# The key cache read one batch at a time in 4 KB runs, in place of two interleaved batches in 8 KB runs

## The chip, the cores and the metric

The kernel runs on one core of one Trainium2 chip. The metric is the time in microseconds of one execution on the device; lower is better. Each kernel is run several times, and the median is compared.

## The reference

Two transformer-like layers are applied twice, with the same weights both times, to four single-token rows `x` of 512 numbers (B = 4, one query position, 32 query heads in 8 groups, head size 128). Of the cache of 8,192 positions only the last W = 2,048 are used.

```python
def _A_ref(x, k_cache, v_cache, wq, wo):
    q = (x @ wq).reshape(B, Sq, Hq, Dh)            # then (B, Hq, Sq, Dh)
    k = jnp.repeat(k_cache[:, :, Sk - W:, :], rep, axis=1)
    v = jnp.repeat(v_cache[:, :, Sk - W:, :], rep, axis=1)
    scores = jnp.einsum("bhqd,bhkd->bhqk", q, k) * (Dh ** -0.5)
    p = _softmax(scores, axis=-1)
    o = jnp.einsum("bhqk,bhkd->bhqd", p, v)
    return o.transpose(0, 2, 1, 3).reshape(B, Sq, Hq * Dh) @ wo

def _B_ref(x, w_gate, w_up, w_down):
    h = _sigmoid(x @ w_gate) * (x @ w_up)
    return h @ w_down

x = x + _A_ref(_layernorm(x), k_cache, v_cache, wq, wo)
x = x + _B_ref(_layernorm(x), w_gate, w_up, w_down)
x = x + _A_ref(_layernorm(x), k_cache, v_cache, wq, wo)
x = x + _B_ref(_layernorm(x), w_gate, w_up, w_down)
```

For one (batch, head group) pair the used part of K, and likewise of V, is 2,048 x 128 numbers in bf16, 512 KB, contiguous in the device's memory. There are 32 such pairs. wq is 512 x 4096 (4 MB), wo 4096 x 512 (4 MB), the three GLU weights 512 x 1792 each (1.8 MB).

## The kernel before

**Memory.** One big tile, `arena`, is cut into NS = 50 slots of 128 partitions x 2,048 bf16 (512 KB each). A slot holds one (batch, head) block of K or V, or a chunk of a weight. `_SlotPool` hands out free slots in the order in which they were released. The list `loads` holds the transfers to come in their fixed order; `fill()` issues them as long as slots are free, and `done(name)` releases a slot after its last use. Every transfer is issued by SyncE through one line (`dma`, L372), in one queue. Its completion is signalled on one of 24 semaphores in turn, so a transfer also waits for the transfer 24 places earlier.

**Order of the loads.** wq first (four transfers of 1 MB, whole rows of 8 KB, into pairs of slots), then K of the first two units, then for each unit K of the unit two ahead, its wo chunk and its four V blocks. After the eight units come the GLU weights, wq again in 512 KB chunks, V again in reverse order of the units (29 of 32 blocks, since three are kept), and the GLU weights again. K stays in its slots from the first attention to the second, and so do the eight chunks of wo.

**A unit** is one head group with its four batches; there are eight units in each attention. For a unit, `front` does the following. In the first attention only, `k_transpose` (L664 to L670) turns each K slot in place on VectorE, in 32 x 32 blocks of 4-byte words. `softmax_unit` then spreads q into a block form (`q_unit`, L643), computes the scores on TensorE (L689: 16 matmuls of 512 columns, four for each batch, the batches in four groups of 32 columns of the array), takes maxima on VectorE (L697 to L703), and applies the exponential on ScalarE into `prow` (L706). `turn_p` permutes the rows with a matmul (L715), copies them on ScalarE (L717) and transposes on VectorE (L721). `pv_unit` (L755) multiplies with V, 16 matmuls for each V block, and `wo_unit` (L785) with wo. `front` runs two units ahead of `pv_unit`. In the second attention the units run in reverse order, and K's four slots are released right after each unit's scores.

**K before.** Slots 0 to 31 are set aside for K: `pool.free` starts at 32 (L353), head h has slots 4h to 4h+3 (`kpair`, L408), and K needs no slot from the pool, so that `take_k` (L383) issues a K load at once when it is the next in the list. `load_k` (L412) makes two transfers for each head, one for each pair of batches:

```python
src = A_k[2 * bp:2 * bp + 2, h, SK - W:SK, :].rearrange("b (p j) d -> p b (j d)", p=64)
dma("K%d_%d" % (h, bp), kpair(h, bp), src, ..., rate="bw_8k")
```

The even partitions of a pair of slots thus hold one batch and the odd ones the other, each partition 32 consecutive positions (8 KB). The matmuls at L689 pick one batch out of the transposed pair (`b % 2`) with a step of four bf16; the exponential (L706) and the copy (L717) use access patterns that bring the positions back into the order in which V lies (V: 16 consecutive positions in each partition, 4 KB).

**Order of the instructions.** `_schedule` (L86) builds each engine's order from estimated durations and dependencies (its table `tm` has a rate for 8 KB runs and one for 4 KB runs), and `_assign_sync` (L174) sets the semaphore waits.

Of the kernel before, what the change touches and what calls it, by code (L numbers as in the profile page):

```python
# [6 lines left out]
F32 = mybir.dt.float32  # L7
# [265 lines left out]
def build(nc, A_x, A_k, A_v, A_wq, A_wo, B_wg, B_wu, B_wd, out, cfg=None):  # L273
# [40 lines left out]
    with es:  # L314
# [35 lines left out]

        P = _Plan()
        pool = _SlotPool(NS)
        pool.free = list(range(4 * HKV, NS))  # L353
        SB = (0, 1)
        PB = 2
        OBS = (3, 4)
# [23 lines left out]
        loads = []  # L380
        where = {}

        def take_k():  # L383
            while loads and loads[0][0][0] == "K":
                loads.pop(0)[1](None)

        def take_load():
            take_k()
            name, emit = loads.pop(0)
            s = pool.alloc()  # L390
            where[name] = s
            emit(s)

        def fill():
            take_k()
            while loads and pool.free:
                take_load()
                take_k()

        def need(name):  # L400
            while name not in where:
# [2 lines left out]

        def done(name):
            pool.release(where.pop(name))

        def kpair(h, bp):  # L408
            o = (4 * h + 2 * bp) * SLOT
            return arena[:, o:o + 2 * SLOT]  # L410

        def load_k(h):  # L412

            where[("K", h)] = h
            for bp in range(2):
                src = A_k[2 * bp:2 * bp + 2, h, SK - W:SK, :].rearrange("b (p j) d -> p b (j d)", p=64)
                dma("K%d_%d" % (h, bp), kpair(h, bp), src, w=[("slot", 4 * h + 2 * bp + i) for i in range(2)],
                    rate="bw_8k")

        def load_kv(name, cache, b, h):  # L420
            loads.append((name, lambda s: dma(str(name), slot_ap(s), kv_d(cache, b, h), w=[("slot", s)])))
# [55 lines left out]

        def load_wq_rows(c):
            def emit(s):
                assert pool.alloc() == s + 1 and s >= 4 * HKV  # L480
# [181 lines left out]
            return [[(h, b) for h in range(u * nh, (u + 1) * nh) for b in g] for u in range(HKV // nh)]  # L662

        def k_transpose(pairs):  # L664
            h = pairs[0][0]
            need(("K", h))
            for t in range(4):
                v32 = slot_ap(4 * h + t).bitcast(F32)
                P.op("vector", "T%d_%d" % (h, t), c_dve(1024), lambda v, v32=v32: v.transpose(v32, v32),  # L669
                     r=[("slot", 4 * h + t)], w=[("slot", 4 * h + t)])  # L670

        ucount = [0]

        def softmax_unit(tag, pairs):
            u = ucount[0]
            ucount[0] += 1
            k2 = u % 2
            bank = SB[k2]
            ob = OBS[k2]
            hk = pairs[0][0]  # L680
            q_unit(tag, int(tag[0]), pairs[0][0], k2)

            def e_s(pe):
                last = None
                for cp in range(4):
                    for gi, (h, b) in enumerate(pairs):
                        kt = kpair(hk, b // 2).rearrange("p (j c x i t) -> p c t i j x", c=2, x=16, i=2, t=2)
                        q0 = ((k2 * NB + b) * 4 + cp) * NR
                        last = pe.matmul(ps[32 * gi:32 * gi + NR, bank, :], qbd[:, q0:q0 + NR],  # L689
                                         kt[:, cp // 2, cp % 2, b % 2, :, :], start=(cp == 0), stop=(cp == 3))  # L690
                return last
            P.op("tensor", "S" + tag, 16 * tm["pe_row"], e_s,
                 r=[("slot", 4 * hk + t) for t in range(4)] + [("q", k2, a) for a in range(4)],
                 w=[("pss", k2)], banks=(bank,))
            mk = mxt[:, k2 * 32:(k2 + 1) * 32]
            P.op("vector", "mx" + tag, c_dve(512),
                 lambda v: v.tensor_reduce(nmax[:, k2:k2 + 1], ps[:, bank, :], AXX, ALU.max),  # L697
                 r=[("pss", k2)], w=[("mx", k2)], banks=(bank,))
            P.op("vector", "mk" + tag, tm["dve_small"],
                 lambda v: v.tensor_scalar(mk, maskr[:, :], nmax[:, k2:k2 + 1], None, ALU.add),  # L700
                 r=[("mx", k2), ("maskr",)], w=[("mk", k2)])
            P.op("vector", "nm" + tag, tm["dve_small"],
                 lambda v: v.tensor_reduce(nmax[:, 2 + k2:3 + k2], mk, AXX, ALU.max, negate=True, apply_transpose=True),  # L703
                 r=[("mk", k2)], w=[("nm", k2)])
            P.op("scalar", "ex" + tag, c_act(512) + 200.0,
                 lambda a: a.activation(prow[:, :].rearrange("p (m x t) -> p m x t", x=16, t=2),  # L706
                                        ps[:, bank, :].rearrange("p (m t x) -> p m x t", x=16, t=2), ACTF.Exp, bias=nmax[:, 2 + k2:3 + k2], scale=1.0,
                                        accum_out=psm[:, k2:k2 + 1]),
                 r=[("pss", k2)] + [("nm", k2)], w=[("prow",), ("psm", k2)], banks=(bank,))
            return k2  # L710

        def turn_p(tag, k2):
            ob = OBS[k2]
            P.op("tensor", "pp" + tag, tm["pe_sq"],
                 lambda pe: pe.matmul(ps[:, PB, :], perm[:, :], prow[:, :], start=True, stop=True),  # L715
                 r=[("prow",), ("perm",)], w=[("ppb",)], banks=(PB,))
            P.op("scalar", "pc" + tag, c_act(512), lambda a: a.copy(prow[:, :].rearrange("p (m y t) -> p m y t", y=2, t=2),  # L717
                                  ps[:, PB, :].rearrange("p (y m t) -> p m y t", y=2, t=2)),
                 r=[("ppb",)], w=[("prow",)], banks=(PB,))
            P.op("vector", "pt" + tag, c_dve(256),  # L720
                 lambda v: v.transpose(ebuf[:, k2 * 256:(k2 + 1) * 256], prow[:, :].bitcast(F32)),  # L721
                 r=[("prow",)], w=[("e", k2)])
# [71 lines left out]
        def attn(L, gi_, wb):  # L794
# [218 lines left out]
```

## Time and profile before

| | |
|---|---|
| median of 4 runs | 189.49 us (188.82 to 190.07) |
| the profiled execution, its own time | 188.62 us |
| span of that execution, first to last instruction | 186.8 us |
| bytes moved | 72.65 MB, mean 389 GB/s |
| K: 16 transfers of 1,024 KB, to landing (median) | 14.8 us |
| V: 61 transfers of 512 KB, to landing (median) | 14.9 us |
| VectorE K transposes (L669), 32 | 38.0 us, 1,219 ns each |
| TensorE score matmuls (L689), 256 | 32.4 us, 632 ns each |
| ScalarE exponentials (L706) and copies (L717), 16 each | 687 ns and 585 ns each |
| TensorE clock granted, mean | 0.705 |

The profile is one execution. The row of 40 slices shows each engine's busy share in tenths, the DMA row the mean busy share of the sixteen DMA engines, and the row below it the rate in GB/s. A group's line gives the source line, engine, operation, output and input, shape and count, then busy time and mean duration, then the engine's idle time before it and what ended that. Durations of matmuls that run in several column groups at once overlap.

### The profile page before, as it was taken

To read this page: it belongs to the slowest core of one execution; us is meant where nothing else is said; L and a number is where in the kernel's file an instruction comes from. 1 tells how busy PE (TensorE), PEld (TensorE's weight loads), DVE (VectorE), ACT (ScalarE), POOL (GpSimd) and SP (SyncE) were. 2 spreads that over 40 slices of the span, in tenths; PEclk is the share of its full clock that TensorE was granted. 3 is DMA by queue.
4 is the path that set the end of the run, shared out by engine and by line. 5 is a ranking of instruction groups with operands and counts; after the bars stand their busy time and mean duration, and the time that the engine had idled before them with its cause. 6 is when DMAs were issued, how large, how long until landed. Compare 5 with 4: busy or idle time off the path is not lost.

```text
span 186.8 us, 4440 instructions
## 1 busy us (share of the span) xinstructions
PE 101.7 (54%) x1920; PEld 56.5 (30%) x1920; DVE 86.2 (46%) x215; ACT 32.7 (18%) x95; POOL 13.9 (7%) x73
## 2 busy tenths in 40 slices
PE   0433406456607163171644346455989999956543
PEld 0101002312404132040334331321355555655122
DVE  6109999268583854738510031123584443311211
ACT  2000021223303003020020001001463333210200
POOL 3000001101101001010010000000121111100000
PEclk9999996885556758585585555555999699675555
DMA  4999999999999999999999999999999999999990
GB/s 162 419 423 430 424 408 396 422 387 415 408 394 427 384 417 408 398 423 388 396 402 387 405 409 366 405 369 410 409 412 404 406 412 403 408 405 408 403 379 24
DMA packets 20532, 72.65 MB, mean 389 GB/s; under 512 B 1944, under 2 KB 6048, under 8 KB 17952
## 3 DMA queue, kind: packets, MB, share of 16 engines
q1 hardware_dynamic: 20512, 72.37, 97.9%
q8 instruction: 15, 0.25, 0.5%
q14 instruction: 5, 0.04, 0.1%
HBM read 72.36 MB, written 0.00 MB: 387 GB/s over the span
## 4 chain that ended last, share of the span: by engine, by line
DMA 38%; SPq 32%; PE 18%; DVE 6%; issue 2%; ACT 2%; ACTq 0%
SPq L372 32%; DMA arena<-in_A_k_cache_dram 16%; DMA arena<-in_B_w_down_dram 11%; PE ps L689 9%; DMA arena<-in_A_v_cache_dram 6%; DMA arena<-in_A_wq_dram 4%; PE ps L755 3%; DVE arena L669 3%; ACT prow L706 1%; PE ps L715 1%; DVE nmax L697 1%; PE ps L785 1%; PE ps L845 1%; PE ps L877 1%; PE ps L615 1%
## 5 line engine op out<-in xcount | busy, mean ns | idle before, releaser
L689 PE MATMUL ps<-arena,qbd 128*16 128x512 bf16 x256 | 32.4, 632 | 26.7 <-DVE arena L669 21.9
L669 DVE STREAM_TRANSPOSE arena<-arena 128x1024 f32<-128x1024 f32 x32 | 38.0, 1219 | 2.8 <-DMA arena<-in_A_k_cache_dram 2.6
L755 PE MATMUL ps<-ebuf,arena 128*128 128x4 bf16 x1024 | 32.2, 165 | 11.1 <-DMA arena<-in_A_v_cache_dram 10.6
L755 PEld LDWEIGHTS ps<-ebuf,arena 128*128 128x128 bf16 x1024 | 29.7, 100 | 19.1 <-DMA arena<-in_A_v_cache_dram 13.0
L689 PEld LDWEIGHTS ps<-arena,qbd 128*16 128x16 bf16 x256 | 6.7, 99 | 40.2 <-DVE arena L669 22.4
L697 DVE TENSOR_REDUCE nmax<-ps 128x1 f32<-128x512 f32 x16 | 11.0, 685 | 16.2 <-PE ps L689 16.2
L706 ACT ACTIVATE prow<-ps,nmax 128x512 bf16<-128x512 f32 x16 | 11.0, 687 | 36.3 <-DVE nmax L703 26.4
L767 DVE TENSOR_TENSOR onb<-ps,rinv 128x16 bf16<-128x16 f32 x16 | 3.1, 195 | 30.8 <-PE ps L755 30.7
L656 ACT CAST qbd<-ps 32x64 bf16<-32x64 f32 x32 | 6.5, 204 | 55.1 <-DVE qbd L653 35.8
L725 POOL CAST s<-psm 128x1 bf16<-128x1 f32 x16 | 3.0, 186 | 143.7 <-ACT prow L706 143.7
L715 PE MATMUL ps<-prow,perm 128*128 128x512 bf16 x16 | 6.8, 428 | 12.3 <-ACT prow L706 12.1
L615 PE MATMUL ps<-arena,xn 128*4 128x512 bf16 x64 | 8.2, 580 | 8.3 <-DMA arena<-in_A_wq_dram 5.4
L717 ACT CAST prow<-ps 128x512 bf16<-128x512 f32 x16 | 9.4, 585 | 8.7 <-PE ps L715 8.7
L845 PE MATMUL ps<-arena,xn 128*4 128x448 bf16 x64 | 7.3, 556 | 6.1 <-DMA arena<-in_B_w_up_dram 3.3
L721 DVE STREAM_TRANSPOSE ebuf<-prow 128x256 f32<-128x256 f32 x16 | 7.1, 442 | 7.6 <-ACT prow L717 7.5
L785 PE MATMUL ps<-onb,arena 128*128 128x4 bf16 x256 | 9.1, 165 | 2.8 <-issue 1.7
L785 PEld LDWEIGHTS ps<-onb,arena 128*128 128x128 bf16 x256 | 8.0, 100 | 3.3 <-issue 2.9
L653 DVE CAST qbd<-ps 32x64 bf16<-32x64 f32 x32 | 6.7, 210 | 3.8 <-ACT qbd L656 2.5
L623 DVE STREAM_TRANSPOSE ebuf<-ps 128x512 f32<-128x512 f32 x4 | 2.9, 714 | 10.3 <-PE ps L615 10.1
L582 ACT ACTIVATE lnv<-lnv 128x4 f32<-128x4 f32 x4 | 0.8, 206 | 38.1 <-DVE lnv L579 38.1
L852 DVE STREAM_TRANSPOSE ebuf<-ps 128x448 f32<-128x448 f32 x4 | 2.6, 650 | 9.9 <-PE ps L845 9.9
L877 PE MATMUL ps<-hT,arena 128*128 128x4 bf16 x112 | 4.2, 167 | 4.9 <-DVE hT L867 2.5
(55 smaller groups left out, 61.0 us busy)
## 6 DMA issues: line engine op xcount, KB each, us to landing
arena<-in_A_v_cache_dram SPq DMA_DIRECT2D x61, 512.0 KB, 14.9
arena<-in_A_k_cache_dram SPq DMA_DIRECT2D x16, 1024.0 KB, 14.8
arena<-in_A_wq_dram SPq DMA_DIRECT2D x4, 1024.0 KB, 8.0
arena<-in_A_wo_dram SPq DMA_DIRECT2D x8, 512.0 KB, 15.5
arena<-in_A_wq_dram SPq DMA_DIRECT2D x8, 512.0 KB, 7.9
arena<-in_B_w_gate_dram SPq DMA_DIRECT2D x8, 448.0 KB, 13.9
arena<-in_B_w_up_dram SPq DMA_DIRECT2D x8, 448.0 KB, 13.4
arena<-in_B_w_down_dram SPq DMA_DIRECT2D x6, 512.0 KB, 7.1
```

Source lines behind the costliest of these rows:

```text
L372: o = P.op("sync", name, 0.0, lambda e, dst=dst, src=src: e.dma_start(dst, src), r=r, w=w, dma_bytes=nbytes, dma_rate=tm[rate])
L615: last = pe.matmul(ps[32 * hh:32 * hh + NB, qb, :], xn[:, c * NB:(c + 1) * NB], slot_ap(s)[:, hh * 512:(hh + 1) * 512], start=(c == 0), st ...
L669: P.op("vector", "T%d_%d" % (h, t), c_dve(1024), lambda v, v32=v32: v.transpose(v32, v32), r=[("slot", 4 * h + t)], w=[("slot", 4 * h + t)])
L689: last = pe.matmul(ps[32 * gi:32 * gi + NR, bank, :], qbd[:, q0:q0 + NR], kt[:, cp // 2, cp % 2, b % 2, :, :], start=(cp == 0), stop=(cp = ...
L697: lambda v: v.tensor_reduce(nmax[:, k2:k2 + 1], ps[:, bank, :], AXX, ALU.max),
L706: lambda a: a.activation(prow[:, :].rearrange("p (m x t) -> p m x t", x=16, t=2), ps[:, bank, :].rearrange("p (m t x) -> p m x t", x=16, t ...
L715: lambda pe: pe.matmul(ps[:, PB, :], perm[:, :], prow[:, :], start=True, stop=True),
L717: P.op("scalar", "pc" + tag, c_act(512), lambda a: a.copy(prow[:, :].rearrange("p (m y t) -> p m y t", y=2, t=2), ps[:, PB, :].rearrange(" ...
L721: lambda v: v.transpose(ebuf[:, k2 * 256:(k2 + 1) * 256], prow[:, :].bitcast(F32)),
L755: last = pe.matmul(ps[:, ob, gi * REP:(gi + 1) * REP], src[:, j * 128:(j + 1) * 128], ev[:, j % 2, j // 2, gi * REP:(gi + 1) * REP], start ...
L785: last = pe.matmul(ps[:, wb, c * nb:(c + 1) * nb], slot_ap(s)[:, r_ * D + c * 128:r_ * D + (c + 1) * 128], ov[:, o0:o0 + nb], start=(first ...
L845: last = pe.matmul(ps[32 * g:32 * g + NB, SB[n], 0:NF], xn[:, c * NB:(c + 1) * NB], slot_ap(s)[:, g * NF:(g + 1) * NF], start=(c == 0), st ...
```

## The change

K is handled as V is: one transfer of 512 KB for each (batch, head) pair, 16 consecutive positions (4 KB) in each of 128 partitions, into one slot taken from the common pool when the load's turn comes. The 32 set-aside slots, `take_k`, `kpair` and `load_k` go; all 50 slots are in the pool from the start. The order of the loads is the same, with four K transfers of a unit where there were two. `k_transpose` works on the same number of slots. The score matmuls read a step of two bf16 from one slot, the exponential writes in steps of two, and the copy after the row permutation becomes plain. In the second attention the four slots of a unit are released at the same point as before.

```diff
-        pool.free = list(range(4 * HKV, NS))
...
-        def load_k(h):
-
-            where[("K", h)] = h
-            for bp in range(2):
-                src = A_k[2 * bp:2 * bp + 2, h, SK - W:SK, :].rearrange("b (p j) d -> p b (j d)", p=64)
-                dma("K%d_%d" % (h, bp), kpair(h, bp), src, w=[("slot", 4 * h + 2 * bp + i) for i in range(2)],
-                    rate="bw_8k")
...
         def k_transpose(pairs):
-            h = pairs[0][0]
-            need(("K", h))
-            for t in range(4):
-                v32 = slot_ap(4 * h + t).bitcast(F32)
-                P.op("vector", "T%d_%d" % (h, t), c_dve(1024), lambda v, v32=v32: v.transpose(v32, v32),
-                     r=[("slot", 4 * h + t)], w=[("slot", 4 * h + t)])
+            for (h, b) in pairs:
+                s = need(("K", h, b))
+                v32 = slot_ap(s).bitcast(F32)
+                P.op("vector", "T%d_%d" % (h, b), c_dve(1024), lambda v, v32=v32: v.transpose(v32, v32),
+                     r=[("slot", s)], w=[("slot", s)])
...
-                        kt = kpair(hk, b // 2).rearrange("p (j c x i t) -> p c t i j x", c=2, x=16, i=2, t=2)
+                        kt = slot_ap(ks[gi]).rearrange("p (j c k t) -> p c t j k", c=2, k=32, t=2)
                         q0 = ((k2 * NB + b) * 4 + cp) * NR
                         last = pe.matmul(ps[32 * gi:32 * gi + NR, bank, :], qbd[:, q0:q0 + NR],
-                                         kt[:, cp // 2, cp % 2, b % 2, :, :], start=(cp == 0), stop=(cp == 3))
+                                         kt[:, cp // 2, cp % 2, :, :], start=(cp == 0), stop=(cp == 3))
...
-                 lambda a: a.activation(prow[:, :].rearrange("p (m x t) -> p m x t", x=16, t=2),
-                                        ps[:, bank, :].rearrange("p (m t x) -> p m x t", x=16, t=2), ACTF.Exp, bias=nmax[:, 2 + k2:3 + k2], scale=1.0,
+                 lambda a: a.activation(prow[:, :].rearrange("p (j k t) -> p j t k", k=32, t=2),
+                                        ps[:, bank, :].rearrange("p (j t k) -> p j t k", k=32, t=2), ACTF.Exp, bias=nmax[:, 2 + k2:3 + k2], scale=1.0,
...
-            P.op("scalar", "pc" + tag, c_act(512), lambda a: a.copy(prow[:, :].rearrange("p (m y t) -> p m y t", y=2, t=2),
-                                  ps[:, PB, :].rearrange("p (y m t) -> p m y t", y=2, t=2)),
+            P.op("scalar", "pc" + tag, c_act(512), lambda a: a.copy(prow[:, :], ps[:, PB, :]),
...
-                    for t in range(4):
-                        pool.release(4 * us[ui][0][0] + t)
+                    for p in us[ui]:
+                        done(("K",) + p)
...
-            for u in us[0:2]:
-                loads.append((("K", u[0][0]), lambda _, h=u[0][0]: load_k(h)))
+            for (h, b) in us[0] + us[1]:
+                load_kv(("K", h, b), A_k, b, h)
             for ui, pairs in enumerate(us):
                 if ui + 2 < len(us):
-                    loads.append((("K", us[ui + 2][0][0]), lambda _, h=us[ui + 2][0][0]: load_k(h)))
+                    for (h, b) in us[ui + 2]:
+                        load_kv(("K", h, b), A_k, b, h)
```

The new loads use the function that V's loads had already:

```python
def load_kv(name, cache, b, h):
    loads.append((name, lambda s: dma(str(name), slot_ap(s), kv_d(cache, b, h), w=[("slot", s)])))
```

with `kv_d` (L310) giving `cache[b, h, SK - W:SK, :]` as 128 partitions of 16 positions.

More of the change, by code (lines that the diff above doesn't have):

```diff
@@ L381, in build @@
         where = {}
-        def take_k():
-            while loads and loads[0][0][0] == "K":
-                loads.pop(0)[1](None)
         def take_load():
-            take_k()
             name, emit = loads.pop(0)
@@ L394, in fill @@
         def fill():
-            take_k()
             while loads and pool.free:
                 take_load()
-                take_k()
         def need(name):
@@ L406, in done @@
             pool.release(where.pop(name))
-        def kpair(h, bp):
-            o = (4 * h + 2 * bp) * SLOT
-            return arena[:, o:o + 2 * SLOT]
-        def load_k(h):
-            where[("K", h)] = h
-            for bp in range(2):
-                src = A_k[2 * bp:2 * bp + 2, h, SK - W:SK, :].rearrange("b (p j) d -> p b (j d)", p=64)
-                dma("K%d_%d" % (h, bp), kpair(h, bp), src, w=[("slot", 4 * h + 2 * bp + i) for i in range(2)],
-                    rate="bw_8k")
         def load_kv(name, cache, b, h):
@@ L479, in emit @@
             def emit(s):
-                assert pool.alloc() == s + 1 and s >= 4 * HKV
+                assert pool.alloc() == s + 1
                 where[(("wq", c, 1), 0)] = s + 1
@@ L679, in softmax_unit @@
             ob = OBS[k2]
-            hk = pairs[0][0]
+            ks = [where[("K", h, b)] for (h, b) in pairs]
             q_unit(tag, int(tag[0]), pairs[0][0], k2)
@@ L686, in e_s @@
                     for gi, (h, b) in enumerate(pairs):
-                        kt = kpair(hk, b // 2).rearrange("p (j c x i t) -> p c t i j x", c=2, x=16, i=2, t=2)
+                        kt = slot_ap(ks[gi]).rearrange("p (j c k t) -> p c t j k", c=2, k=32, t=2)
                         q0 = ((k2 * NB + b) * 4 + cp) * NR
                         last = pe.matmul(ps[32 * gi:32 * gi + NR, bank, :], qbd[:, q0:q0 + NR],
-                                         kt[:, cp // 2, cp % 2, b % 2, :, :], start=(cp == 0), stop=(cp == 3))
+                                         kt[:, cp // 2, cp % 2, :, :], start=(cp == 0), stop=(cp == 3))
                 return last
             P.op("tensor", "S" + tag, 16 * tm["pe_row"], e_s,
-                 r=[("slot", 4 * hk + t) for t in range(4)] + [("q", k2, a) for a in range(4)],
+                 r=[("slot", s) for s in ks] + [("q", k2, a) for a in range(4)],
                  w=[("pss", k2)], banks=(bank,))
```

## The prediction

> **What bounds the kernel now.** I read first the engines' busy shares and the 40 slices. No compute engine is busy for more than 54% of the span, while the row of the DMA engines stands at 9 from the second slice to the one before the last, with rates between 366 and 430 GB/s.
>
> ```profile
> PE 101.7 (54%) x1920; PEld 56.5 (30%) x1920; DVE 86.2 (46%) x215; ACT 32.7 (18%) x95; POOL 13.9 (7%) x73
> ...
> DMA  4999999999999999999999999999999999999990
> GB/s 162 419 423 430 424 408 396 422 387 415 408 394 427 384 417 408 398 423 388 396 402 387 405 409 366 405 369 410 409 412 404 406 412 403 408 405 408 403 379 24
> ...
> q1 hardware_dynamic: 20512, 72.37, 97.9%
> ```
>
> The third row says the same for the whole span: the packets of SyncE's queue fill 97.9% of sixteen engines' time. So the end is set by how many bytes pass and at which rate. The rate must then be read by kind of run, from windows in which one kind is alone. The columns are: stretch, length, busy time of PE, PEld, DVE, ACT, POOL, granted clock, DMA share, GB/s.
>
> ```profile
> 10.00:24.00 14.00, 4.89 (x64) 1.09 (x64) 9.52 (x13) 0.41 (x2) 0.00 (x0) 1.00 1.01 426
> 26.00:107.00 81.00, 37.82 (x752) 22.78 (x752) 44.41 (x84) 13.76 (x38) 6.04 (x32) 0.64 1.03 403
> 107.00:126.00 19.00, 9.35 (x136) 4.82 (x136) 4.22 (x20) 1.57 (x7) 0.00 (x0) 0.50 1.01 388
> 130.00:166.00 36.00, 34.45 (x732) 19.96 (x728) 17.36 (x63) 13.86 (x39) 6.09 (x32) 0.88 1.03 408
> 134.00:136.00 2.00, 2.00 (x21) 0.47 (x17) 1.67 (x5) 1.06 (x4) 0.75 (x4) 1.00 1.04 416
> ```
>
> From 10 to 24 us only 8 KB runs land (the end of wq and the first six K transfers): 426 GB/s. From 130 to 166 us nearly all is V in 4 KB runs: 408 GB/s. Between 26 and 107 us K, V and wo (1 KB runs) are mixed: 403. From 107 to 126 us, around the first GLU, few slots are free and the rate falls to 388. The share is at 1 in all of them: the engines are never empty, even in the stage from 130 us where PE is busy for 34.45 of 36 us.
>
> Last I read the issues and the end of the chain of waits:
>
> ```profile
> arena<-in_A_v_cache_dram SPq DMA_DIRECT2D x61, 512.0 KB, 14.9
> arena<-in_A_k_cache_dram SPq DMA_DIRECT2D x16, 1024.0 KB, 14.8
> ...
> arena<-in_A_wo_dram SPq DMA_DIRECT2D x8, 512.0 KB, 15.5
> ```
> ```profile
> 168.15 14.62 DMA arena<-in_B_w_down_dram
> 182.81 0.59 PE ps L877 x16
> 183.44 0.39 PE ps L877 x8
> 184.09 0.60 PE ps L940 x4
> 184.71 0.41 DVE prow L943
> ```
>
> A transfer lands some 15 us after its issue, so about 15 x 0.408 = 6 MB stand in the queue. The span ends with the last w_down transfer, about 4 us of fixed work behind it. A microsecond more of DMA time anywhere ahead moves the end by a microsecond.
>
> **The change, part by part.** (1) K comes in 32 transfers of 512 KB in 4 KB runs, not 16 of 1,024 KB in 8 KB runs. The bytes stay: 16 x 1,024 KB = 16.78 MB. At 426 GB/s they take 39.4 us, at V's 408 they take 41.1: +1.7 us. No trace shows K in 4 KB runs, so bounds: V's best short window above has 416 GB/s, 40.3 us, +0.9; the mixed stretch, which wo's 1 KB runs slow down, has 403, 41.6 us, +2.2. I take 408, since V's transfers have the same size, the same runs and the same kind of source. These rates include the completion of each transfer, so the doubled number is in them.
>
> The Trainium skill has two rules here. "DMA: Bandwidth & Descriptors", section "Rules for kernel authors", wants at least 1 MiB a transfer, and the fit of the same page's "Anatomy of one DMA", made for GpSimd's queue, is 2.0 us + bytes / 436 GB/s: 32 x 3.2 - 16 x 4.4 = some 32 us more if each stood alone. V's row speaks against it: 512 KB transfers at 408 GB/s, a queue of 6 MB in front. The section "Why small descriptors are slow" of that page charges about 3 cycles of 32 B beats for each packet: 2 x (128 + 3) against 256 + 3 cycles, 1.2%, an estimate of +0.5 us, below what the windows show.
>
> (2) SyncE issues 16 more transfers. A K issue takes 624 ns in the median, so 16 x 0.62 = 10 us of SyncE's time. In the first stretch six of them push wo's issue from 7.2 to about 11 us, and the first V behind it; that V's issue stalled from 7.9 to 15.8 us on the full queue anyway, so nothing starves. Later an issue takes longer only because the queue is full. Cost 0; without the cover of the 6 MB, 10 us. The new transfers also wait for the transfer 24 places earlier, which a queue of about 12 transfers has long passed: 0.
>
> (3) K takes slots from the common pool when it is loaded. Before, slots 0 to 31 were set aside and 18 were left for all else. Now up to 50 are open early, but from the last K load on it is 32 K and 18 others as before, at the GLU too. So SyncE's early waits for a slot (15.6 us for L755) shrink, and go to waits for the queue. Worth 0 for a DMA row at share 1; bounded in rival D.
>
> (4) A transpose (L669, 32 x 1,219 ns, unchanged in number and shape) can start when its own 512 KB has landed. Two transposes stood behind the last 1 MB of a unit, now one: the score matmuls can start 1.2 us earlier against the landing. They are followed by PV matmuls that wait for V (10.6 us at L755), so this moves idle time on PE. 0, at best 8 units x 1.2 us if DMA were not the bound.
>
> (5) Access patterns. The score matmuls L689 (16 a unit) read every second bf16 instead of every fourth. Four in four column groups take 2.03 / 4 = 0.51 us at that step; L615, without any step, takes 0.44 to 0.60 for four: no price of the step in sight, so 0; bounds from these rows 16 units x 4 x -0.07 to +0.09, or -4 to +6 us of PE. The exponential L706 (687 ns) writes in steps rather than reading in steps, the copy L717 (585 ns) becomes plain; bounds for each from the two rows, -0.1 to +0.1 us x 16. All of it lies under DMA: in the second attention PE needs 4.6 us a unit (S at 140.06, 144.68 and 149.29 us), the DMA 4 x 0.524 / 0.408 = 5.1, so a unit has 0.5 us of cover. 0 taken.
>
> Sum: +1.7 us on the span, 186.8 to 188.5. The profiled execution lasted 188.62 us, 1.8 more than its span, and becomes 190.3. The median of the runs shown is 189.49, 0.9 above that execution, so the forecast is 191.2 us.
>
> **The rivals.** A is the forecast, own range +0.9 to +2.2: 190.4 to 191.7.
>
> B, the run length hardly matters: what made 426 GB/s is the quiet start without wo and without many completions. Then K in 4 KB runs passes there at nearly the old rate. For it: only 6 of 16 K transfers stand in that window. Against it: slices further on in which K prevails still reach 423 and 427, which V's stretch never does. Take 10/16 of the K bytes as unaffected: 6/16 x 1.7 = +0.6, 190.1 us, no change.
>
> C, K's doubled transfers thin the queue. If the queue counts descriptors and not bytes, K in flight halves, and the mixed stretch could pass at the 388 GB/s of the stretch around the first GLU, where in-flight work is also small: 16.78 / 388 = 43.2 us, +3.9, 193.4 us. Against it: V has this size and run now, and lands 14.9 us after issue at 408. It decides if the K stretches fall under 400.
>
> D, the time does not rise: wider pool and finer landing feed the DMA earlier between 26 and 126 us. What could be regained: in 26 to 107, at 426 for the 10 remaining K transfers (10.5 MB, 24.6 us) and 408 for the rest (81 x 0.403 - 10.5 = 22.1 MB, 54.2 us), 78.8 us would do, 2.2 less; around the GLU 19 x (408 - 388) / 408 = 0.9. Together 3.1, net 1.7 - 3.1 = -1.4, 188.1 us; from 1.7 regained on it is not slower. Against it: the share is 1.03 there, and wo's 1 KB runs explain the first part; the second has the same free slots as before.
>
> **How the numbers follow.** A 0.68, B 0.17, C 0.08, D 0.07. About 0.5% (0.95 us) is what a measurement of this kernel can tell from no change. Slower takes nearly all of A and C, 0.75; A's lowest part, B and the less-than-full part of D make 0.19 for no change; D in full makes 0.06. The time is A's, 191.2 us. The range goes down to just under B, 189.9, and up past A's 191.7 by the 0.3% by which single runs stand from their median, 192.3; C and D lie outside.
>
> **What would show it.** Right: packets under 8 KB rise by 2 x 2,048 = 4,096; the window of the first K loads moves at about 408 and not 426; the DMA share stays at 1; the last w_down lands 1.7 us later with the same 4 us behind it; L669 and L689 keep their means. Wrong: 10 to 24 us at 420 or more (B), K stretches under 400 (C), the first GLU starting no later than at 111.8 us (D), or a DMA share clearly below 1 from 130 us on with PE full, which would mean that the access patterns of (5) have a price after all.

## The result, and the profile after

| | before | after |
|---|---|---|
| median of all its runs in the comparison | 189.28 us (66 runs) | 189.85 us (42 runs) |
| ratio after / before, 95% interval | | 1.0033, 1.0023 to 1.0043 |
| profiled execution, its own time | 188.62 us | 190.84 us |
| its span | 186.8 us | 189.1 us |

The changed kernel is slower by 0.33%, which is 0.6 us (0.4 to 0.8). The forecast was 191.2 us, +1.7. The two profiled executions lie 2.2 us apart, because the one of before stands 0.7 us under its median and the one of after 1.0 us over it. One pair of profiles therefore cannot give the size of this change; further profiles of both kernels follow below.

First the page of the changed kernel: engines, the forty slices, the DMA queue, the groups that answer to the lines of before, and the issues. L668 is the line of the score matmuls here, L648 that of K's transposes, L733 that of the matmuls with V, L685 that of the exponential.

```profile
PE 103.3 (55%) x1920; PEld 57.8 (31%) x1920; DVE 86.2 (46%) x215; ACT 34.3 (18%) x95; POOL 13.9 (7%) x73
...
DMA  5999999999999999999999999999999999999980
GB/s 165 421 420 415 408 403 393 411 388 411 397 395 412 385 413 399 400 405 392 396 400 391 405 409 354 390 384 411 409 408 407 404 409 409 405 407 404 408 318 5
DMA packets 22836, 72.66 MB, mean 384 GB/s; under 512 B 2200, under 2 KB 6304, under 8 KB 22304
...
q1 hardware_dynamic: 22816, 72.37, 97.8%
...
L733 PE MATMUL ps<-ebuf,arena 128*128 128x4 bf16 x1024 | 34.5, 167 | 17.6 <-DMA arena<-in_A_v_cache_dram 17.4
L668 PE MATMUL ps<-arena,qbd 128*16 128x512 bf16 x256 | 28.8, 595 | 22.6 <-DVE arena L648 18.8
L648 DVE STREAM_TRANSPOSE arena<-arena 128x1024 f32<-128x1024 f32 x32 | 38.5, 1222 | 0.8 <-DMA arena<-in_A_k_cache_dram 0.4
...
L685 ACT ACTIVATE prow<-ps,nmax 128x512 bf16<-128x512 f32 x16 | 13.3, 829 | 28.6 <-DVE nmax L682 27.2
...
L696 ACT CAST prow<-ps 128x512 bf16<-128x512 f32 x16 | 9.4, 586 | 10.7 <-PE ps L694 10.7
...
arena<-in_A_v_cache_dram SPq DMA_DIRECT2D x61, 512.0 KB, 12.6
arena<-in_A_k_cache_dram SPq DMA_DIRECT2D x32, 512.0 KB, 13.5
```

The same lines of the page of before:

```profile
DMA packets 20532, 72.65 MB, mean 389 GB/s; under 512 B 1944, under 2 KB 6048, under 8 KB 17952
...
L689 PE MATMUL ps<-arena,qbd 128*16 128x512 bf16 x256 | 32.4, 632 | 26.7 <-DVE arena L669 21.9
L669 DVE STREAM_TRANSPOSE arena<-arena 128x1024 f32<-128x1024 f32 x32 | 38.0, 1219 | 2.8 <-DMA arena<-in_A_k_cache_dram 2.6
L755 PE MATMUL ps<-ebuf,arena 128*128 128x4 bf16 x1024 | 32.2, 165 | 11.1 <-DMA arena<-in_A_v_cache_dram 10.6
...
L706 ACT ACTIVATE prow<-ps,nmax 128x512 bf16<-128x512 f32 x16 | 11.0, 687 | 36.3 <-DVE nmax L703 26.4
```

The reader sees the same kernel, still filled by DMA from the second slice on. The packets under 8 KB rise from 17,952 to 22,304: 4,096 runs of K, which were not under 8 KB before, and 256 small packets (the "under 512 B" count, 1,944 to 2,200), 16 for each of the 16 transfers more. The slices two to five, where K's first transfers land, no longer reach 430. The 25th to 27th slices, around the first GLU, fall to 354, 390 and 384. The transfers wait less in the queue (V 12.6 us to landing, 14.9 before); this goes with the run length and not with the size of a transfer, as the kernel with 1,024 KB transfers below shows.

The windows that the prediction read, now of the changed kernel (stretch, length, busy time of PE, PEld, DVE, ACT, POOL, granted clock, DMA share, GB/s):

```profile
10.00:24.00 14.00, 4.68 (x64) 1.08 (x64) 9.74 (x13) 0.41 (x2) 0.00 (x0) 1.00 1.02 413
26.00:107.00 81.00, 39.05 (x736) 23.15 (x736) 44.17 (x85) 14.52 (x38) 6.09 (x32) 1.00 1.04 399
107.00:126.00 19.00, 8.81 (x144) 5.23 (x148) 4.23 (x20) 1.57 (x7) 0.00 (x0) 1.00 1.00 384
126.00:170.00 44.00, 38.75 (x807) 22.21 (x801) 18.78 (x67) 14.99 (x40) 6.09 (x32) 0.68 1.03 408
```

From 10 to 24 us the rate falls from 426 to 413, not to 408. From 26 to 107 it falls from 403 to 399. The second attention is unchanged at 408 (from 126 to 170 us; the row of before stands in the last section). So K's runs do cost time, but less than the forecast's 426 against 408.

To put the stretches of many executions side by side I counted, in each trace, when the n-th megabyte of SyncE's queue had landed. The order of the loads is the same in all these kernels, so the first 41.9 MB are wq, K, V and wo of the first attention, 43 to 51 MB are the GLU weights and the second read of wq around the first GLU, and 51 to 72.3 MB are V of the second attention and most of the last GLU weights. The last column is the time from there to the end of the span. Times in us, lowest and highest where there are several profiles:

```
kernel (profiles)                        1-41.9 MB      43-51 MB      51-72.3 MB    rest
before (4)                            100.48-100.56  20.63-21.44   52.89-53.34  4.43-4.63
after, one with other addresses (5)   101.64-101.73  20.34-20.89   53.01-53.18  4.38-5.29
4 KB runs, set-aside slots (3)        101.58-101.64  20.47-21.33   53.13-53.22  4.61-5.11
4 KB runs, 1,024 KB a transfer (1)       101.66         21.02         53.17       5.18
2 KB runs, 1,024 KB a transfer (1)       104.06         20.63         53.09       4.58
before, ten free slots (1)               100.50         19.73           -          -
after, ten free slots (1)                101.75         19.69           -          -
set-aside, ten free slots (1)            101.63         19.70           -          -
```

The first column is the run length, and it repeats within 0.2 us: 8 KB runs 100.5, 4 KB runs 101.65, so +1.15 us. The second and the last column are where executions of one kernel differ most, by up to 0.9 us. The high time of the first profile of the changed kernel stands in its last column (5.29 us).

On the mean the five profiles of the second row span 188.2 us and the four of before 187.1: 1.0 us apart, where the medians of all runs are 0.6 apart. So in the profiles most of the first column's 1.15 us reaches the end.

### The profile page after: what moved, and what is told of

It is laid out like the page before. It is cut to its first block, busy times and chain, and to the rows that moved or that the text cites. A ratio compares the mean times of both kernels' runs of the same rounds, so it can differ in the third digit from the quotient of the medians.

```text
span 189.1 us, 4461 instructions
## 1 busy us (share of the span) xinstructions
PE 103.3 (55%) x1920; PEld 57.8 (31%) x1920; DVE 86.2 (46%) x215; ACT 34.3 (18%) x95; POOL 13.9 (7%) x73
## 2 busy tenths in 40 slices
DMA packets 22836, 72.66 MB, mean 384 GB/s; under 512 B 2200, under 2 KB 6304, under 8 KB 22304
## 3 DMA queue, kind: packets, MB, share of 16 engines
q1 hardware_dynamic: 22816, 72.37, 97.8%
## 4 chain that ended last, share of the span: by engine, by line
DMA 51%; SPq 28%; PE 12%; DVE 4%; issue 2%; ACT 2%; ACTq 0%
DMA arena<-in_A_v_cache_dram 28%; SPq L371 28%; DMA arena<-in_B_w_down_dram 11%; DMA arena<-in_A_k_cache_dram 7%; PE ps L668 5%; DMA arena<-in_A_wq_dram 4%; PE ps L733 2%; PE ps L823 1%; PE ps L694 1%; DVE nmax L676 1%; ACT prow L685 1%; PE ps L763 1%; DVE arena L648 1%; PE ps L595 1%; PE ps L855 1%
## 5 line engine op out<-in xcount | busy, mean ns | idle before, releaser
L733 PE MATMUL ps<-ebuf,arena 128*128 128x4 bf16 x1024 | 34.5, 167 | 17.6 <-DMA arena<-in_A_v_cache_dram 17.4
L668 PE MATMUL ps<-arena,qbd 128*16 128x512 bf16 x256 | 28.8, 595 | 22.6 <-DVE arena L648 18.8
L733 PEld LDWEIGHTS ps<-ebuf,arena 128*128 128x128 bf16 x1024 | 31.4, 104 | 26.4 <-DMA arena<-in_A_v_cache_dram 24.3
L648 DVE STREAM_TRANSPOSE arena<-arena 128x1024 f32<-128x1024 f32 x32 | 38.5, 1222 | 0.8 <-DMA arena<-in_A_k_cache_dram 0.4
L685 ACT ACTIVATE prow<-ps,nmax 128x512 bf16<-128x512 f32 x16 | 13.3, 829 | 28.6 <-DVE nmax L682 27.2
L676 DVE TENSOR_REDUCE nmax<-ps 128x1 f32<-128x512 f32 x16 | 11.0, 686 | 15.0 <-PE ps L668 14.9
L668 PEld LDWEIGHTS ps<-arena,qbd 128*16 128x16 bf16 x256 | 6.2, 108 | 35.5 <-DVE arena L648 19.1
L694 PE MATMUL ps<-prow,perm 128*128 128x512 bf16 x16 | 9.0, 564 | 9.3 <-ACT prow L685 8.2
## 6 DMA issues: line engine op xcount, KB each, us to landing
arena<-in_A_v_cache_dram SPq DMA_DIRECT2D x61, 512.0 KB, 12.6
```

Source lines behind the costliest of these rows:

```text
L648: P.op("vector", "T%d_%d" % (h, b), c_dve(1024), lambda v, v32=v32: v.transpose(v32, v32), r=[("slot", s)], w=[("slot", s)])
L685: lambda a: a.activation(prow[:, :].rearrange("p (j k t) -> p j t k", k=32, t=2), ps[:, bank, :].rearrange("p (j t k) -> p j t k", k=32, t ...
L733: last = pe.matmul(ps[:, ob, gi * REP:(gi + 1) * REP], src[:, j * 128:(j + 1) * 128], ev[:, j % 2, j // 2, gi * REP:(gi + 1) * REP], start ...
```

## The experiments

The theories: the forecast's (T1: run length alone, 1.7 us), one that the common pool or the finer landing pays part of a 1.7 us cost back (T2), and one that the run length is worth less than the forecast said (T3). Ratios are to the kernel before, run on the same chip; the experiments ran on several chips, and only ratios compare across them. Where an expectation numbers its theories, the numbers are its own.

**The kernels as they are, again.** No edit.

> The kernel before, unchanged, for a second profiled execution and the spread of its runs. Both theories: ratio 1.000 within 0.2%. What it tells: the first profiled execution (188.62 us) lies 0.7 us below the kernel's median. If the DMA stream (run lengths) alone sets the time, a second profile has the same rates in 10 to 24 us (426 GB/s) and 26 to 107 us (403) and differs only in its last microseconds; if the rates in the long stretches themselves vary by 1%, the run-length term read from one profile was noise of that size.

> The changed kernel, unchanged, on the same chip as the others. Both theories: ratio 1.003, about +0.6 us. What it tells: its first profiled execution (190.84 us) lies 1.0 us above its median. If that excess is a disturbance, the profile here ends near a span of 188.0 and the loss against the first profile is seen in the last part of the span, not in the K stretches; if the K stretches are at 413 and 399 GB/s again, the run-length cost is real and something else pays it back.

Before: 189.29 us, ratio 1.0008 (0.999 to 1.0027). After: 190.08 us, 1.0057 (1.0037 to 1.0077). The windows of both second profiles, the kernel before first:

```profile
10.00:24.00 14.00, 4.84 (x64) 1.09 (x64) 9.55 (x13) 0.41 (x2) 0.00 (x0) 1.00 1.01 427
26.00:107.00 81.00, 35.49 (x745) 22.55 (x752) 44.46 (x84) 13.79 (x38) 6.08 (x32) 0.64 1.03 403
107.00:126.00 19.00, 9.42 (x142) 4.97 (x139) 4.23 (x20) 1.57 (x7) 0.00 (x0) 0.50 0.98 371
```
```profile
10.00:24.00 14.00, 4.65 (x64) 1.08 (x64) 9.71 (x13) 0.41 (x2) 0.00 (x0) 1.00 1.02 413
26.00:107.00 81.00, 35.42 (x728) 23.19 (x736) 44.28 (x85) 14.52 (x38) 6.09 (x32) 1.00 1.04 400
107.00:126.00 19.00, 9.21 (x148) 5.26 (x148) 4.22 (x20) 1.57 (x7) 0.00 (x0) 1.00 1.00 380
```

The long stretches repeat to a GB/s. What moves most between executions of the kernel before is the stretch around the first GLU: 388 GB/s in the first profile of before, 371 in this one with the DMA share under 1, which is 0.8 us more for the same 8 MB. The first profile of before was an execution that lost little there. Two more profiles of before:

> The kernel before, a third profile. If it loses more around the first GLU than the changed kernel, that stretch (43 to 51 MB) takes 21 us or more again, and the K stretch (1 to 41.9 MB) 100.5 us; if the loss is the same in both, 20.3 to 20.9 us, and the remaining 0.6 us of difference is then unexplained.

> The kernel before, a fourth profile, with the same two expectations: 21 us or more for the 8 MB around the first GLU if the kernel before loses more there, 20.3 to 20.9 us if not; 100.5 us for the K stretch in either case.

They gave 189.59 us (1.0034, 0.9998 to 1.0071) and 188.85 us (0.9977, 0.994 to 1.0013), with 100.51 and 100.48 us for the first 41.9 MB and 20.84 and 20.63 us around the GLU. So that stretch is not longer in the kernel before by more than its own spread: four values of mean 20.9 against five of mean 20.6 in the changed kernel, and the ranges overlap. By these expectations the remaining half microsecond is unexplained.

**K in 4 KB runs with set-aside slots.** The change without its pool.

```diff
         pool = _SlotPool(NS)
+        pool.free = list(range(4 * HKV, NS))
...
+        def load_k1(b, h):
+            def emit(_):
+                s = 4 * h + b
+                where[("K", h, b)] = s
+                dma("K%d_%d" % (h, b), slot_ap(s), kv_d(A_k, b, h), w=[("slot", s)])
+            loads.append((("K", h, b), emit))
...
-                load_kv(("K", h, b), A_k, b, h)
+                load_k1(b, h)
```

> The change without its pool: K in 4 KB runs, 512 KB a transfer, but slots 0 to 31 set aside for K and 18 for the rest, as before. Theory 1 (the run length costs only about 0.6 us and the pool is worth nothing): ratio 1.003, same as the changed kernel. Theory 2 (the run length costs the forecast 1.7 us and the wider pool pays 1.1 back): ratio 1.009, +1.7 us, and 1.1 us slower than the changed kernel.

Measured 190.57 us, 1.0075 (1.0051 to 1.01), which looked like T2. But its first 41.9 MB took 101.58 us, the same as with the pool, and its excess stood around the first GLU (21.33 us). The instructions of PE, VectorE, ScalarE and GpSimd stand in the same order in both kernels, and only SyncE's early waits differ. It was therefore run twice more, each time beside the changed kernel:

> The changed kernel once more, beside the one with set-aside slots on one chip. If the common pool is worth something, it stands 0.5 us or more ahead of the next run again. If not (the order of the instructions on PE, VectorE and ScalarE is the same in both, and SyncE's early waits differ only where the queue is full), the two agree within 0.2%.

> K in 4 KB runs with set-aside slots, once more. If the common pool is worth something: ratio 1.0075 again, 0.5 us or more behind the changed kernel. If the earlier gap was the spread of the stretch around the first GLU: the same as the changed kernel within 0.2%, both between 1.003 and 1.007.

> The changed kernel on the same chip: 1.0035 to 1.006. A fourth profile of the stretch around the first GLU.

> Set-aside slots and 4 KB runs once more: 1.007 if the gap of half a microsecond to the changed kernel is real, 1.0035 to 1.006 if it was the spread of a few runs.

After: 189.80 us (1.0047, 1.0029 to 1.0066) and 189.95 us (1.0033, 1.0015 to 1.005). Set-aside: 190.38 us (1.0069, 1.0044 to 1.0093), then 189.86 us (1.0027, 1.0008 to 1.0047). In the third comparison, the one with most runs (12 of each), the gap is gone. T2's 1.1 us from the pool falls. The earlier gaps of half a microsecond are within the spread of six to nine runs each; an effect of a tenth or two is not excluded.

**The same slots at other addresses.**

```diff
         pool = _SlotPool(NS)
+        pool.free = list(range(4 * HKV, NS)) + list(range(4 * HKV))
```

> The changed kernel with the common pool's list starting at slot 32, so that every block lies at another address; loads, order and waits are the same. If the place of the slots does not matter: the same as the changed kernel, 1.0035 to 1.006. If the place of the streaming slots makes the gap to the set-aside version: another value, up to 1.0075.

190.09 us, 1.0035 (1.0014 to 1.0055), beside 1.0033 for the changed kernel on that chip: the place of the slots made no difference that can be seen.

**4 KB runs in transfers of 1,024 KB.** To part the run length from the number of transfers.

```diff
-                dma("K%d_%d" % (h, b), slot_ap(s), kv_d(A_k, b, h), w=[("slot", s)])
+                src = A_k[b:b + 2, h, SK - W:SK, :].rearrange("b (p j) d -> p b (j d)", p=128)
+                dst = arena[:, s * SLOT:(s + 2) * SLOT].rearrange("p (b x) -> p b x", b=2)
+                dma("K%d_%d" % (h, b), dst, src, w=[("slot", s), ("slot", s + 1)])
...
```

> As the kernel with set-aside slots, but K in 16 transfers of 1,024 KB, each in 4 KB runs: two batches side by side in two slots. It parts run length from number of transfers. Theory 1 (the run length sets the cost): ratio as with 32 transfers in 4 KB runs, 1.003. Theory 2 (the finer landing of 512 KB transfers pays back 1.1 us of a run-length cost of 1.7): ratio 1.009. Theory 3 (the number of transfers costs, not the run length): ratio 1.000.

190.59 us, 1.0079 (1.0057 to 1.0101); 413 and 399 GB/s in the first two windows, 101.66 us for 41.9 MB. With half the transfers nothing is won against the 1.0075 of 512 KB transfers beside it: the cost belongs to the runs, not to the transfers, and the finer landing pays nothing either. Its issues:

```profile
arena<-in_A_v_cache_dram SPq DMA_DIRECT2D x61, 512.0 KB, 12.8
arena<-in_A_k_cache_dram SPq DMA_DIRECT2D x16, 1024.0 KB, 15.0
```

V lands 12.8 us after its issue, where the same transfers beside 8 KB runs of K took 14.9. A queue that holds a limited number of runs, not of bytes, would do this; what sets it was not tried.

**2 KB runs.** The suspected cost doubled and more.

```diff
-                src = A_k[b:b + 2, h, SK - W:SK, :].rearrange("b (p j) d -> p b (j d)", p=128)
-                dst = arena[:, s * SLOT:(s + 2) * SLOT].rearrange("p (b x) -> p b x", b=2)
+                src = A_k[b:b + 2, h, SK - W:SK, :].rearrange("b (p y j) d -> p y b (j d)", p=128, y=2)
+                dst = arena[:, s * SLOT:(s + 2) * SLOT].rearrange("p (y b x) -> p y b x", b=2, y=2)
...
```

The score matmuls are changed to read K from where it then lies.

> As the 1,024 KB transfers in 4 KB runs with set-aside slots, but each run cut to 2 KB (the halves of a slot pair hold two batches each), so K has 8,192 runs and not 4,096. Theory 1 (a fixed cost for each run, some 1.15 us for 2,048 more runs as the first attention of the changed kernel showed): 4,096 more runs add 2.3 us, ratio 1.020 to the kernel before, with all of it landed by the first GLU. Theory 2 (only the step from 8 to 4 KB mattered): as with 4 KB runs, 1.008.

192.45 us, 1.0172 (1.0145 to 1.0199), and its two windows:

```profile
10.00:24.00 14.00, 4.73 (x64) 1.08 (x64) 9.18 (x12) 0.41 (x2) 0.00 (x0) 1.00 1.03 394
26.00:107.00 81.00, 37.22 (x704) 22.18 (x704) 45.39 (x85) 14.51 (x38) 6.09 (x32) 1.00 1.05 391
```

413 becomes 394, 399 becomes 391, and the first 41.9 MB take 104.06 us, 2.4 more than with 4 KB runs. 4,096 more runs for 2.4 us on sixteen engines are 9.4 ns a run (2.4 x 16 / 4,096); the change's 2,048 more runs for 1.15 us are 9.0 ns. A fixed cost for each run explains both. At the end of the kernel 3.2 of the 3.55 us arrive, a little less than the expectation's 1.020.

**K's transfers alone.** All computation left out.

```diff
...
+        stream("a", 48, e8)
+        stream("b", 96, e4)
+        stream("c", 48, e4p)
...
```

Here `e8` is the load of before, `e4` that of after, and `e4p` the one with 4 KB runs in 1,024 KB.

> Only K's transfers, nothing else: 48 of 1,024 KB in 8 KB runs, then 96 of 512 KB in 4 KB runs, then 48 of 1,024 KB in 4 KB runs (50.3 MB each), then the four rows of x are written out; all computation is left out. The forecast's reading (8 KB runs 426, 4 KB runs 408 GB/s, as V in the second attention): 118, 123 and 123 us for the three parts. The reading from the first attention of the changed kernel (413 GB/s): 118, 122 and 122 us. If the number of transfers counted and not the run length, the second part would be slower than the third.

Windows inside each part (POOL is the only engine listed):

```profile
20.00:110.00 90.00, 0.00 (x0) 1.00 1.01 422
135.00:225.00 90.00, 0.00 (x0) 1.00 1.03 410
260.00:360.00 100.00, 0.00 (x0) 1.00 1.03 410
```

422 against 410, whatever the size of the transfer. For K's 16.78 MB that is 39.8 against 40.9 us: +1.16. This is the run length's price with nothing else in the way (one execution), and it agrees with the first attention's 1.15.

**Ten free slots around the first GLU.** Both kernels with no V block kept, which loads three more blocks and frees three slots there.

```diff
-        KEEP_V = cfg.get("KEEP_V", 3)
+        KEEP_V = cfg.get("KEEP_V", 0)
```

> The kernel before with KEEP_V 0 for 3: no V block is kept, three more are loaded again, and three more slots are free around the first GLU. Three loads of 1.28 us cost 3.9 us; if the stretch around the first GLU loses about 1 us for want of free slots, some of that comes back: ratio 1.015 to 1.020. It is the base for the next run.

> The changed kernel with KEEP_V 0, to be compared with the kernel before with KEEP_V 0. Theory A (the run-length cost of 1.15 us stands at the first GLU, and the stretch around the first GLU, short of slots, gives part of it back): with ten slots free instead of seven there is nothing to give back, and the difference of the two grows to 1.2 us. Theory B (the whole difference is 0.6 us, and one profile of the kernel before lay low): it stays at 0.6 us. Theory C (the forecast): 1.7 us.

> K in 4 KB runs with set-aside slots, KEEP_V 0. If the pool is worth nothing by itself: the same as the changed kernel with KEEP_V 0, ratio 1.022, 193.4 us, with the same narrow spread. If the pool pays half a microsecond wherever it is used: 193.9 us.

Before: 192.38 us (1.0169, 1.0143 to 1.0195). After: 193.40 us (1.0222, 1.0196 to 1.0248). Set-aside slots with 4 KB runs: 193.56 us (1.0213, 1.0188 to 1.0238). The stretch around the first GLU in the first two:

```profile
107.00:126.00 19.00, 9.58 (x136) 4.82 (x136) 4.22 (x20) 1.57 (x7) 0.00 (x0) 0.50 1.03 407
```
```profile
107.00:126.00 19.00, 9.25 (x148) 5.23 (x148) 4.22 (x20) 1.57 (x7) 0.00 (x0) 1.00 1.03 406
```

With ten slots the rate holds at 407 and 406, and the 8 MB take 19.7 us in all three kernels, where seven slots took 20.3 to 21.4. The runs then lie close together: 192.24 to 192.63 us for before, 193.33 to 193.45 for after. The difference of these two, run on one chip, is 193.40 - 192.38 = 1.0 us, so most of the run length's cost comes through (their first 41.9 MB differ by 1.25 us); of that expectation's theories A (1.2 us) is nearest. The set-aside version ran on another chip, so its time does not compare with these two; by the ratios it stands 0.4%, some 0.8 us, above the kernel before with ten slots. What this says of the kernels as they are: the stretch with few free slots is a good part of what spreads the executions. Whether the missing half microsecond is lost there is not shown.

**One slot more.** KEEP_V 2 in the kernel before.

> The kernel before with KEEP_V 2 for 3: one V block more is loaded (1.28 us), and eight slots instead of seven are free around the first GLU. If the loss of that stretch (about 1 us against ten slots) goes with the first slot added: ratio 1.000 to 1.002 and a narrow spread of the runs. If it needs all three: ratio 1.005.

190.85 us, 1.0101 (1.0079 to 1.0124): neither expectation. In its profile the rate from 107 to 126 us rises to 405, but from 126 to 132 us it is 384 where before had 409, so part of the loss may only have moved. One more block of V at 1.28 us is not earned back.

**The step of the score matmuls.** In the kernel before, one slot read in steps of two; the scores then mix two batches.

```diff
-                        kt = kpair(hk, b // 2).rearrange("p (j c x i t) -> p c t i j x", c=2, x=16, i=2, t=2)
+                        kt = slot_ap(4 * hk + b).rearrange("p (j c k t) -> p c t j k", c=2, k=32, t=2)
```

> The kernel before, with the score matmuls reading one slot in steps of two bf16, as the changed kernel does, in place of a pair of slots in steps of four; the scores then mix positions of two batches. Loads, order and everything else as before. Forecast part (5): the time stays at 1.000, since PE is under the DMA. The granted TensorE clock was 0.68 to 0.71 in all runs of the kernel before and 0.87 to 0.88 in all with K in 4 KB or 2 KB runs: if the step of the score matmuls makes that difference, it is about 0.87 here; if the copies, the exponential or the transfers make it, about 0.69.

One run, 190.12 us. Ten of the eleven runs of before on that chip lie between 188.49 and 189.43 us, one at 191.71; the 66 of the comparison reach from 188.54 to 190.96. One run cannot tell whether the time changed. Its windows of the first attention and of the GLU:

```profile
26.00:107.00 81.00, 35.80 (x745) 23.67 (x752) 44.58 (x84) 13.78 (x38) 6.09 (x32) 1.00 1.03 403
107.00:126.00 19.00, 8.29 (x133) 4.67 (x132) 4.24 (x20) 1.57 (x7) 0.00 (x0) 1.00 0.99 366
```

In the first attention the rate is still 403, as with 8 KB runs, but the granted clock is 1.00 where before had 0.64. So the clock goes with the step, and it leaves this stretch's time alone (100.5 us for the first 41.9 MB). Around the GLU, where the kernel before has a clock of 0.50 and the changed one 1.00, the rate here is 366 GB/s at 1.00, the lowest of the profiles shown: the one run gives no sign that the clock makes the half microsecond.

None of the versions tried is quicker than the kernel before.

## Why the prediction was wrong

The direction was right, though the prediction would have called a change of 0.33% no change by its own limit of 0.5%. The forecast of 191.2 us lies 1.35 us over the measured 189.85. Of that, 0.2 us is the base: the forecast started from a median of four runs, 189.49, and 66 runs give 189.28. Another 0.55 us is the price of the run length, 1.7 against 1.15. The remaining 0.6 us is cost that is seen in the first attention and, in the medians, not at the end.

**What bounds the kernel: right.** The DMA queue filled 97.8% of the sixteen engines' time after the change, and the first attention moved by what its runs cost while the waits of PE and VectorE changed around it. The first GLU began at 113.1 us (111.8 before), 1.3 later. The last w_down landed at 184.4 us on the mean of the profiles, 183.1 before: 1.3 later, not 1.7, with 3.4 to 4.1 us behind it.

**Part (1), the term that was mis-sized.** The prediction took K in 4 KB runs at "V's 408" and 8 KB runs at 426, +1.7 us. Measured: +1.15 us by the first GLU, and 1.16 us in the stream of K alone. The mechanism was right, and the two windows were not like for like. The 426 stood at the quick start of the kernel, where 4 KB runs make 413; the 408 stood in the busy second attention. In the stream alone the pair is 422 and 410. The direct comparison, in the same stretch, was not in the trace of before; of the bounds, the lower one of 0.9 us, from V's best short window, was the nearer.

Of the two rules weighed there from "DMA: Bandwidth & Descriptors" of the Trainium skill, the one on transfers of at least 1 MiB ("Rules for kernel authors") made no difference in this queue: 410 GB/s with 512 KB and with 1,024 KB alike. The cost of some 3 cycles for each packet ("Why small descriptors are slow") gave an estimate of 0.5 us and had the right form, a fixed cost for each run; the runs show 1.15 us, so more than twice that.

**"A microsecond more of DMA time anywhere ahead moves the end by a microsecond": not confirmed in full, and the second term that was off.** With ten free slots 1.0 us of 1.25 arrived. With seven, the medians of the comparison differ by 0.6 us (0.4 to 0.8). The full 1.15 us would be a ratio of 1.0061. It lies inside the intervals of two of the later comparisons (1.0057 and 1.0047) and outside those of the larger ones (1.0033, and 1.0033 again with 12 runs). The nine profiles are 1.0 us apart on the mean. So the shortfall is clear in the largest comparison and not seen in all of them.

The prediction had seen the stretch from 107 to 126 us at 388 GB/s, and rival D counted it as a loss of 0.9 us, the same in both kernels. It is not fixed: the 8 MB there took from 20.3 to 21.4 us from one execution to another, about twice the 0.6 us by which the medians differ. The means over the profiles (20.9 before, 20.6 after) go the right way to explain half of the missing 0.5 us, but the ranges overlap. That the kernel before loses more there is thus not settled, and the cause of the shortfall stays open. The pool, the slot addresses, the size of the transfers and the granted clock were tried, and none of them accounts for it as far as the runs tell.

**The base.** The profiled execution of before, from which the sums were made, was among those that lost least in that stretch, but the fourth profile lost as little there (20.63 us) and took 0.45 us more. Moving the sum to the median, as was done, is right for the level; four runs left the level 0.2 us too high, and say nothing of the spread of one stretch.

**Part (2), 16 more issues: right.** SyncE needed 11.6 us for K's first twelve issues and reached wo's at 14.9 us (7.2 before; the estimate was 11), since issues began to stall with the eighth. The DMA share stood at 1.02 from 10 to 24 us, so no DMA time was lost.

**Part (3), the pool: right as far as seen**, worth nothing in the third comparison (1.0033 against 1.0027 without it) nor with ten slots (1.0222 against 1.0213). SyncE's waits for the matmuls with V shrank from 15.6 to 9.3 us, as said.

**Part (4), the finer landing: right.** VectorE's wait for K fell from 2.6 to 0.4 us and PE's wait for the transposes from 21.9 to 18.8, while PE's wait for V grew from 10.6 to 17.4. The idle time moved, as said.

**Part (5): 0 in time as far as the runs tell, but a bound and a sign failed.** L685, the exponential, went from 687 to 829 ns, +0.14 us where the bound was 0.1, and the copy stayed at 586. Both lie under DMA. The score matmuls were to keep their mean and went from 632 to 595 ns; with the old exponential in place the step of two gave 591 ns, so it goes with the step.

**The rivals.** B's 190.1 us was nearest to the result, but that was luck: it let 4 KB runs pass at nearly the old rate at the start, and they fell to 413. It was right in part, for the place counts too: of the 18 GB/s between 426 and 408, 13 go with the run length and 5 with the place. C's sign, K stretches under 400, came true by the letter at 399 (400 in the repeat), and V's earlier landing fits its thinner queue; its price did not come: the rate stayed far from 388, and the DMA share in that window was 1.04. D's mechanism, the pool and the finer landing feeding the DMA, is out; whether its place, the stretch around the GLU, is where the rest was lost is not settled.

## What to carry to other kernels

Where DMA fills the span, price a change of run length as a fixed cost for each run: here 9 ns on each of sixteen engines, from 8 KB to 2 KB, whatever the size of a transfer. Take such a price from two windows that differ in nothing else, or from a stream of the transfers alone; two windows of one kernel carry their surroundings with them.

Before booking a small loss onto the end of the kernel, look for a stretch where the queue runs thin. With few free slots it varied here by about a microsecond, so one profile is no base; a few profiles, or a version with more slots, show what is left. Count the runs behind the base too: four of them were 0.2 us off.

## What the hardware showed that I had not expected

Reading the score matmuls' moving operand (K) in steps of four bf16 went with a granted TensorE clock of 0.64 from 26 to 107 us, and in steps of two with 1.00, the loads and the other instructions being the same. The mean over the span was 0.67 to 0.72 in all runs with the step of four and 0.86 to 0.89 in all with the step of two. In the second attention there is no such rule. The window from 126 to 170 us of the first profile of before, whose counterpart after the change has 0.68:

```profile
126.00:170.00 44.00, 38.58 (x824) 22.47 (x820) 18.74 (x67) 14.16 (x40) 6.09 (x32) 0.81 1.03 408
```
The second profiles have 0.73 before and 0.66 after, and the kernel before with the step of two 0.72. No time was seen to follow from the clock in these stretches, and why the step should go with it was not tried.
